# Keeping weight differences in device memory instead of making them again for every chunk

## The chip, the core and the metric

The kernel runs on one core of one Trainium2 chip. The metric is the device time of one execution in microseconds (us). The kernel before takes 1067.56 us, the median of three runs (1067.38 to 1067.63).

## The reference, cut to what matters

Linear attention without a softmax, with a root-mean-square norm per head, is followed by a gated feed-forward block. All tensors are float32 except the three weight matrices, which arrive as float64 and are converted at the start. There are 8 batches of 8 heads, 576 positions each, heads of width 64; the feed-forward block sees 4608 tokens of width 512 and has 1536 hidden units.

```python
kv  = np.einsum('bhsd,bhse->bhde', k, v)
out = np.einsum('bhsd,bhde->bhse', q, kv)
out = out / np.sqrt(np.mean(out * out, axis=-1, keepdims=True) + 1e-06) * g_norm
x   = out.transpose(0, 2, 1, 3).reshape(4608, 512)
gate = 1.0 / (1.0 + np.exp(-(x @ w_gate)))
val  = x @ w_val
return gate * val @ w_out
```

## The kernel before

The 4608 tokens are worked through in nine chunks of 512, numbered 0 to 8. Chunk 0 uses ordinary matrix products while the weights arrive and are converted. Chunks 1 to 8 use a Strassen-Winograd scheme in both layers: seven products of half size in place of eight, in exchange for sums and differences of the operands. TensorE makes the products, VectorE and ScalarE combine them, and GpSimd makes the differences of the weights. The attention of a later batch is fed in between the products of the first layer.

The first layer of a chunk has six rounds (`NF2 = 6`). Round f treats two blocks of 128 hidden units, f and f + 6, here called `one` and `two`. The differences of the gate and value weights of a round (`tw`, four tiles per block, and `tw2`, four small ones for an inner Strassen step) are made by GpSimd in the round before, and this is done again in every chunk although the weights never change:

```python
def w_sums2(f):
    bf, bg = w["wg", f], w["wg", f + NF2]
    b11, b12, b21, b22 = bf[:, NK], bg[:, NK], bf[:, NK + 1], bg[:, NK + 1]
    for i, in0, in1 in ((1, b12, b11), (2, b22, 1), (4, b21, 2), (3, b22, b12)):
        tw2[i] = sums.tile([P, P], FP32, tag=f"tx{i}", name=f"tx{i}", bufs=1)
        nc.gpsimd.tensor_tensor(out=tw2[i], in0=in0, in1=..., op=ALU.subtract)

def w_sum(f, i):
    ...
    tw[f, i] = sums.tile([P, NK, P], FP32, tag=f"tw{i}", name=f"tw{i}")      # two buffers per tag
    nc.gpsimd.tensor_tensor(out=tw[f, i], in0=b[in0], in1=..., op=ALU.subtract)
```

A round, with the vector work left out (`pN` is one product of two 128x128x256 float32 matmuls, `small` one matmul of 128 columns; `tw` and `tw2` are what each reads; `slot()` is a place where a step of the attention is fed in):

```python
p1(one); p1(two); slot()                          # weights themselves
small(..., ones[:, NK]); small(..., ones[:, NK + 1])
p6(one)                                           # tw[f, 2]
small(..., tw2[2]); small(..., tw2[4])
p6(two); slot()                                   # tw[f + 6, 2]
small(..., tw2[3])
p5(one); slot()                                   # tw[f, 1]
p7(one)                                           # tw[f, 3]
small(..., tw2[1]); slot()
p7(two); p5(two); slot()                          # tw[f + 6, 3], tw[f + 6, 1]
if more:                                          # the next round's differences
    for k_ in (1, 2):
        w_sum(n, k_); w_sum(n + NF2, k_)
    w_sums2(n)
    for i in (n, n + NF2): w_sum(i, 3)
p4(one); small(...); p4(two); slot()              # tw[f, 4], tw[f + 6, 4]
if more:
    for i in (n, n + NF2): w_sum(i, 4)
p3(one); p3(two); slot()                          # weights themselves
```

The buffers are just enough for one round: the differences of the next round go into the places that `p5`, `p6`, `p7` and `p4` of this round have just read.

All loads and stores go through one queue, that of SyncE, in program order. Two of them matter here: the keys and values of a later batch, loaded at the end of each chunk's second layer, and the queries, each loaded when the queries before have been turned.

```python
def load_late(b):                                 # called after the second layer of chunk c, for b = c + 2
    if b >= B: return
    for n in range(NHP):                          # 4 x (k, v): 8 loads of 256 KB
        for name, src in (("k", k), ("v", v)):
            nc.sync.dma_start(out=..., in_=src[b, 2 * n:2 * n + 2, 0:S4]...)
    for i, src in enumerate((k, v)):              # 4 loads of 64 KB
        for r in range(2):
            nc.sync.dma_start(out=..., in_=src[b, NHP * r:NHP * r + NHP, S4:S]...)
```

Of the kernel before, what the change touches and what calls it, by code (L numbers as in the profile page):

```python
# [10 lines left out]
FP32 = mybir.dt.float32  # L11
# [4 lines left out]
ALU = mybir.AluOpType  # L16
# [4 lines left out]
def kernel(  # L21
# [11 lines left out]
    nc = tc.nc  # L33
# [4 lines left out]
    P = 128  # L38
# [89 lines left out]
    staged, w = {}, {}  # L128
# [206 lines left out]
    def slot():  # L335
        if fill:
            fill.popleft()()
# [138 lines left out]
    def gv_tile(c, f):  # L476
        gv[c, f] = hp.tile([P, G], FP32, tag="gv", name="gv")
        return gv[c, f]

    def sg_tile():  # L480
        return sb.tile([P, G], FP32, tag="sg", name="sg", bufs=5)
# [29 lines left out]
    def bank(i):  # L511
        return (psum_mm if i < 2 else psum).tile([P, 512], FP32, tag=f"mm{i}", name="mm")
# [15 lines left out]
    def take():  # L528
        i = free.popleft()
        return i, bank(i)[:, 0:GH]  # L530

    def give(i):
        free.append(i)
# [67 lines left out]
    for token in order.split():  # L601
        name = token.rstrip("0123456789.")
        n = [int(i) for i in token[len(name):].split(".")]
        f = n[0]
# [68 lines left out]
    NK = NMT // 2  # L673
    NF2 = NFT // 2
# [3 lines left out]
    sx, tw, s12, s4 = {}, {}, {}, {}  # L678


    sx2, tw2 = {}, {}
# [3 lines left out]
    def quarters(c):  # L685
        return {(i, j): xT[c][:, NK * (j - 1):NK * j, GH * (i - 1):GH * i] for i in (1, 2) for j in (1, 2)}
# [18 lines left out]
            lambda: tt(out=s[:, 2], in0=a12, in1=s[:, 1], op=ALU.subtract),  # L705
        ]

    def w_sums2(f):

        bf, bg = w["wg", f], w["wg", f + NF2]  # L710
        b11, b12, b21, b22 = bf[:, NK], bg[:, NK], bf[:, NK + 1], bg[:, NK + 1]
        for i, in0, in1 in ((1, b12, b11), (2, b22, 1), (4, b21, 2), (3, b22, b12)):
            tw2[i] = sums.tile([P, P], FP32, tag=f"tx{i}", name=f"tx{i}", bufs=1)
            nc.gpsimd.tensor_tensor(out=tw2[i], in0=in0, in1=tw2[in1] if isinstance(in1, int) else in1,  # L714
                                    op=ALU.subtract)

    def w_sum(f, i):
        b = {(j, n): w[name, f][:, NK * (j - 1):NK * j, :] for n, name in ((1, "wg"), (2, "wv")) for j in (1, 2)}
        tw[f, i] = sums.tile([P, NK, P], FP32, tag=f"tw{i}", name=f"tw{i}")
        in0, in1 = {1: ((1, 2), (1, 1)), 2: ((2, 2), 1), 3: ((2, 2), (1, 2)), 4: ((2, 1), 2)}[i]  # L720
        nc.gpsimd.tensor_tensor(out=tw[f, i], in0=b[in0], in1=b[in1] if isinstance(in1, tuple) else tw[f, in1],  # L721
                                op=ALU.subtract)

    def first_layer_fast(c):
        s, a, s2, ax = sx[c], quarters(c), sx2[c], quarters(c)[1, 2]

        def product(ps, wt, xs, new):
            for m in range(NK):
                nc.tensor.matmul(ps, wt[:, m, :], xs[:, m, :], start=(new and m == 0), stop=(m == NK - 1),  # L729
                                 skip_group_check=True)  # L730

        def small(ps, wt, xs, new):
            nc.tensor.matmul(ps, wt, xs, start=new, stop=True, skip_group_check=True)  # L733


        def p1(d):
            d["ia"], d["pa"] = take()
            product(d["pa"], d["bg"][:, 0:NK], a[1, 1], True)

        def p1_out(d):  # L740
            d["u"] = d["sg"] = sg_tile()
            nc.scalar.copy(out=d["sg"][:, h2], in_=d["pa"])  # L742

        def p6(d):
            d["ib"], d["pb"] = take()
            product(d["pb"], tw[d["f"], 2], s[:, 1], True)
            d["h"] = gv_tile(c, d["f"])
            tt(out=d["h"][:, h1], in0=d["pb"], in1=d["sg"][:, h2], op=ALU.add)  # L748

        def u_sum(d, ps):  # L750

            tt(out=d["h"][:, h2], in0=ps, in1=d.pop("u")[:, h2], op=ALU.add)  # L752
            d["u"] = d["h"]

        def p5(d, i):
            d["ic"], d["pc"] = i, bank(i)[:, 0:GH]
            product(d["pc"], tw[d["f"], 1], s[:, 0], True)
            u_sum(d, d["pc"])

        def p7(d):  # L760
            product(d["pb"], tw[d["f"], 3], a[2, 1], False)
            u_sum(d, d["pb"])

        def p4(d):
            product(d["pb"], tw[d["f"], 4], a[2, 2], False)
            tt(out=d["sg"][:, h2], in0=d["pb"], in1=d["sg"][:, h2], op=ALU.add)  # L766
            nc.scalar.activation(out=d["sg"][:, h2], in_=d["sg"][:, h2], func=AF.Sigmoid)  # L767
            give(d["ib"])

        def p3(d):  # L770
            product(d["pc"], d["bv"][:, NK:], s[:, 2], False)
            tt(out=d["h"][:, h1], in0=d["pc"], in1=d["h"][:, h1], op=ALU.add)
            give(d["ic"])

        def end(d, h):
            tt(out=d["h"][:, h], in0=d["h"][:, h], in1=d["sg"][:, h], op=ALU.mult)  # L776

        for f in range(NF2):
            one, two = ({"f": i, "bg": w["wg", i], "bv": w["wv", i]} for i in (f, f + NF2))
            more = f + 1 < NF2 or c + 1 < NG  # L780
            n = (f + 1) % NF2
            ones, twos = one["bg"], two["bg"]

            p1(one)
            p1_out(one)
            p1(two)
            slot()


            i_d = free[2]  # L790
            del free[2]
            pd = bank(i_d)
            small(pd[:, q1], ones[:, NK], ax[:, 0, q1], True)
            g1 = one["sg"]
            nc.scalar.copy(out=g1[:, q1], in_=pd[:, q1])

            p1_out(two)
            g2 = two["sg"]
            small(one["pa"][:, q1], ones[:, NK + 1], ax[:, 1, q1], False)
            p6(one)  # L800
            small(pd[:, q1], tw2[2], s2[:, 1], False)
            nc.scalar.copy(out=g2[:, q1], in_=pd[:, q1])
            small(one["pa"][:, q2], tw2[4], ax[:, 1, q2], False)
            p6(two)
            slot()
            small(pd[:, q1], tw2[3], ax[:, 0, q2], False)
            nc.scalar.copy(out=g1[:, q2], in_=pd[:, q1])
            nc.scalar.copy(out=g2[:, q2], in_=pd[:, q1])  # L808
            nc.gpsimd.tensor_tensor(out=g2[:, h1], in0=g2[:, h1], in1=g2[:, h2], op=ALU.add)  # L809
            tt(out=g1[:, h1], in0=one["pa"], in1=g1[:, h1], op=ALU.add)  # L810
            nc.scalar.activation(out=g1[:, h1], in_=g1[:, h1], func=AF.Sigmoid)
            p5(one, two["ia"])
            slot()
            p7(one)
            pe = bank(i_d)
            small(pe[:, q1], tw2[1], s2[:, 0], True)
            tt(out=g2[:, q2], in0=pe[:, q1], in1=g2[:, q2], op=ALU.add)
            slot()
            p7(two)
            p5(two, one["ia"])  # L820
            slot()

            if more:
                for k_ in (1, 2):
                    w_sum(n, k_)
                    w_sum(n + NF2, k_)
                w_sums2(n)
                for i in (n, n + NF2):
                    w_sum(i, 3)
            p4(one)  # L830
            small(pe[:, q1], twos[:, NK + 1], s2[:, 2], False)
            tt(out=g2[:, q1], in0=pe[:, q1], in1=g2[:, q1], op=ALU.add)
            nc.scalar.activation(out=g2[:, h1], in_=g2[:, h1], func=AF.Sigmoid)
            p4(two)
            give(i_d)
            slot()
            if more:
                for i in (n, n + NF2):
                    w_sum(i, 4)

            end(one, h2)
            p3(one)
            end(two, h2)
            h_sum(c, f)
            p3(two)
            slot()
            end(one, h1)
            end(two, h1)
            h_sums(c, f)

    def h_sum(c, f):
        one, two = gv[c, f], gv[c, f + NF2]
        s12[c, f] = s = hp.tile([P, G], FP32, tag="gv", name="s12")
        tt(out=s[:, h1], in0=one[:, h2], in1=two[:, h2], op=ALU.add)
# [191 lines left out]
            fill.append(lambda: fill.extendleft(reversed(x_sums(c))))  # L1046

    sums = ctx.enter_context(tc.tile_pool(name="sums", bufs=2, side="right"))
    for n in (1, 2, 3, 4):
        for f in (0, NF2):  # L1050
            w_sum(f, n)
    w_sums2(0)
    fill.extend(x_sums(1))
    for t in range(G // P):
        for f in range(NFT - 2, NFT):
# [23 lines left out]
    for c in range(1, NG):  # L1079
        if c + 1 < B:  # L1080
            steps = feed(c + 1)
            if c == 1:

                i = 4
# [38 lines left out]
```

## Time and profile before

| What | Value |
|---|---|
| Time, median of 3 runs | 1067.56 us |
| Span of the profiled execution | 1066.2 us |
| TensorE busy | 1058.0 us, 99% of the span |
| VectorE busy | 740.6 us, 69% |
| GpSimd busy | 587.5 us, 55% |
| ScalarE busy | 307.2 us, 29% |
| Moved by DMA | 65.05 MB, 61 GB/s over the span |
| Granted TensorE clock | 1.000 |

How to read it: the busy time of TensorE is the union of the intervals of its matmul records. Matmuls are pipelined and their ends are modelled, so a busy share of 99% does not by itself say that nothing waits; the distances between the starts of matmuls do. The chain of waits names what ended last, step by step. A float32 matmul leaves two records in the trace. In the tables by line, the name ahead of `<-` is the tile that is written, the names after it those that are read, and `x` gives the count; tiles of converted weights show under the name `gv` or `w`. SPq is the DMA queue of SyncE.

### The profile page before, as it was taken

The numbers are of one execution on the slowest core, as the hardware profiler recorded it, in microseconds if no ns is written. First come the engines' busy times: TensorE is split into PE (matmuls) and PEld (weight loads), VectorE is DVE, ScalarE is ACT, GpSimd is POOL, SyncE is SP. The second block draws the span as 40 slices with busy tenths as digits, with TensorE's granted clock in tenths as the row PEclk, the third lists the DMA queues.
The fourth block names the chain that finished last, engine by engine and source line by source line (L and its number), as shares of the span: only waits on it lengthen the run. The fifth ranks groups of instructions, "written<-read, shape, count | busy, mean of one in ns | idle before, by whom it ended". The sixth has DMA issues, their size and how long they took to land.

```text
span 1066.2 us, 20718 instructions
## 1 busy us (share of the span) xinstructions
PE 1058.0 (99%) x7766; PEld 887.8 (83%) x7766; DVE 740.6 (69%) x1545; ACT 307.2 (29%) x737; POOL 587.5 (55%) x966
## 2 busy tenths in 40 slices
PE   8999999999999999999999999999999999999998
PEld 7644448888988898889888898889888988898887
DVE  4887776995678647884679467855787477827751
ACT  4654323331243214240333124311432022102210
POOL 0000035878366927784667736792678277847720
PEclk9999999999999999999999999999999999999999
DMA  9944601002400131011301150014000200010001
GB/s 254 263 158 158 239 20 38 12 13 57 141 1 23 43 102 55 23 35 47 117 13 27 41 141 8 16 50 135 14 24 24 62 1 1 1 38 4 1 1 40
DMA packets 70563, 65.05 MB, mean 61 GB/s; under 512 B 25152, under 2 KB 64448, under 8 KB 70464
## 3 DMA queue, kind: packets, MB, share of 16 engines
q1 hardware_dynamic: 70112, 63.66, 21.4%
q8 instruction: 62, 1.02, 0.4%
q14 instruction: 37, 0.30, 0.1%
q10 hardware_dynamic: 352, 0.07, 0.0%
HBM read 47.19 MB, written 9.44 MB: 53 GB/s over the span
## 4 chain that ended last, share of the span: by engine, by line
PE 98%; DMA 1%; SPq 1%; issue 0%; DVE 0%
PE mm L729 47%; PE mm L894 17%; PE mm L557 7%; PE mm L733 7%; PE mm L953 6%; PE mm L654 4%; PE mm L1004 3%; PE at L395 2%; PE at L354 1%; DMA v<-in_v_dram 1%; PE at L557 1%; PE two L261 0%; PE two L291 0%; PE two L318 0%; PE two L272 0%; SPq L87 0%
## 5 line engine op out<-in xcount | busy, mean ns | idle before, releaser
L721 POOL TENSOR_TENSOR tw<-gv 128x256 f32<-128x256 f32 x192 | 158.6, 836 | 258.0 <-DVE w L202 146.1
L729 PE MATMUL mm<-xT,tw 128*128 128x256 f32 x768 | 199.5, 382 | 0.0
L729 PE MATMUL mm<-sx,tw 128*128 128x256 f32 x768 | 197.4, 380 | 0.0
L721 POOL TENSOR_TENSOR tw<-gv,tw 128x256 f32<-128x256 f32 x192 | 153.4, 819 | 0.0
L729 PEld LDWEIGHTS mm<-xT,tw 128*128 128x128 f32 x768 | 136.6, 190 | 19.3 <-issue 3.8
L729 PEld LDWEIGHTS mm<-sx,tw 128*128 128x128 f32 x768 | 134.9, 191 | 12.3
L809 POOL TENSOR_TENSOR sg<-sg 128x256 f32<-128x256 f32 x48 | 35.1, 732 | 166.4 <-ACT sg L808 148.2
L776 DVE TENSOR_TENSOR gv<-gv,sg 128x256 f32<-128x256 f32 x192 | 110.7, 596 | 0.0
L742 ACT COPY sg<-mm 128x256 f32<-128x256 f32 x96 | 36.0, 375 | 242.7 <-PE mm L729 238.8
L729 PE MATMUL mm<-xT,gv 128*128 128x256 f32 x384 | 90.8, 379 | 0.0
L729 PE MATMUL mm<-sx,gv 128*128 128x256 f32 x384 | 90.7, 379 | 0.0
L767 ACT ACTIVATE sg<-sg 128x256 f32<-128x256 f32 x96 | 39.9, 416 | 149.7 <-DVE sg L766 149.7
L729 PEld LDWEIGHTS mm<-sx,gv 128*128 128x128 f32 x384 | 73.0, 190 | 9.9
L729 PEld LDWEIGHTS mm<-xT,gv 128*128 128x128 f32 x384 | 72.3, 190 | 10.0 <-issue 0.5
L557 PE MATMUL mm<-xT,gv 128*128 128x512 f32 x176 | 77.4, 593 | 0.0
L894 PE MATMUL mm<-w,s 128*128 128x256 f32 x336 | 73.7, 379 | 0.0
L894 PEld LDWEIGHTS mm<-w,s 128*128 128x128 f32 x336 | 63.8, 190 | 8.7
L752 DVE TENSOR_TENSOR gv<-mm,sg 128x256 f32<-128x256 f32 x96 | 39.9, 415 | 40.1 <-PE mm L729 39.1
L557 PEld LDWEIGHTS mm<-xT,gv 128*128 128x128 f32 x176 | 32.7, 190 | 37.4 <-issue 35.9
L766 DVE TENSOR_TENSOR sg<-mm,sg 128x256 f32<-128x256 f32 x96 | 40.4, 421 | 33.1 <-PE mm L729 32.9
L748 DVE TENSOR_TENSOR gv<-mm,sg 128x256 f32<-128x256 f32 x96 | 36.5, 411 | 37.6 <-PE mm L729 37.6
L714 POOL TENSOR_TENSOR tx<-gv,tx 128x128 f32<-128x128 f32 x96 | 54.6, 569 | 7.5
(156 smaller groups left out, 1907.5 us busy)
## 6 DMA issues: line engine op xcount, KB each, us to landing
out_dram<-sg SPq DMA_DIRECT2D x110, 64.0 KB, 1.7
q<-in_q_dram SPq DMA_DIRECT2D x24, 288.0 KB, 3.0
st<-in_moe_w_gate_dram SPq DMA_DIRECT2D x12, 512.0 KB, 4.6
st<-in_moe_w_val_dram SPq DMA_DIRECT2D x12, 512.0 KB, 5.6
st<-in_moe_w_out_dram SPq DMA_DIRECT2D x12, 512.0 KB, 4.3
kv<-in_k_dram SPq DMA_DIRECT2D x24, 256.0 KB, 5.0
kv<-in_v_dram SPq DMA_DIRECT2D x24, 256.0 KB, 5.0
xT<-xTs SPq DMA_DIRECT2D x48, 72.0 KB, 2.1
```

What stands on the lines that cost most here:

```text
L557: nc.tensor.matmul(self.ps[i], w[("wg", "wv")[i], self.f][:, m, :], xT[self.c][:, m, :], start=(m == 0), stop=(m == NMT - 1), skip_group_c ...
L654: nc.tensor.matmul(ps[t], gv[0, f][:, P * t:P * t + P], w["wo", f], start=(f == 0), stop=(f == NFT - 1), skip_group_check=True)
L714: nc.gpsimd.tensor_tensor(out=tw2[i], in0=in0, in1=tw2[in1] if isinstance(in1, int) else in1, op=ALU.subtract)
L721: nc.gpsimd.tensor_tensor(out=tw[f, i], in0=b[in0], in1=b[in1] if isinstance(in1, tuple) else tw[f, in1], op=ALU.subtract)
L729: nc.tensor.matmul(ps, wt[:, m, :], xs[:, m, :], start=(new and m == 0), stop=(m == NK - 1), skip_group_check=True)
L733: nc.tensor.matmul(ps, wt, xs, start=new, stop=True, skip_group_check=True)
L752: tt(out=d["h"][:, h2], in0=ps, in1=d.pop("u")[:, h2], op=ALU.add)
L766: tt(out=d["sg"][:, h2], in0=d["pb"], in1=d["sg"][:, h2], op=ALU.add)
L767: nc.scalar.activation(out=d["sg"][:, h2], in_=d["sg"][:, h2], func=AF.Sigmoid)
L776: tt(out=d["h"][:, h], in0=d["h"][:, h], in1=d["sg"][:, h], op=ALU.mult)
L894: nc.tensor.matmul(ps, hs[f], ws[:, f, :], start=(new and f == 0), stop=(f == NF2 - 1), skip_group_check=True)
L953: nc.tensor.matmul(ps, hs[j], ws[j], start=(new and j == 0), stop=(j == N3 - 1), skip_group_check=True)
```

## The change

In chunk 1 the differences are made by GpSimd as before, and each is also stored into device memory (`kept`, `kept2`). In every later chunk the same tiles are filled by a load from there. The two blocks of a round share one tile per kind (256 KB: 128 partitions of 2 KB), and the four inner differences share one (also 256 KB), so that a round needs five loads. The places in the program where the differences are made, and where they are now loaded, are the same, and so is the amount of buffer: two blocks in one tile with one buffer, instead of one block per tile with two. The change takes the repeated work off GpSimd.

```diff
-    def w_sums2(f):
+    def w_sums2(c, f):
+        t = sums.tile([P, 4, P], FP32, tag="tx", name="tx", bufs=1)
+        tw2.update({i: t[:, i - 1] for i in (1, 2, 3, 4)})
+        if c > 1:
+            nc.sync.dma_start(out=t, in_=kept2[f])
+            return
         ...
-            tw2[i] = sums.tile([P, P], FP32, tag=f"tx{i}", name=f"tx{i}", bufs=1)
             nc.gpsimd.tensor_tensor(out=tw2[i], in0=in0, in1=..., op=ALU.subtract)
+        nc.sync.dma_start(out=kept2[f], in_=t)
-    def w_sum(f, i):
-        tw[f, i] = sums.tile([P, NK, P], FP32, tag=f"tw{i}", name=f"tw{i}")
+    def w_sum(c, f, i):
+        t = sums.tile([P, 2, NK, P], FP32, tag=f"tw{i}", name=f"tw{i}", bufs=1)
+        for e in range(2):
+            tw[f + NF2 * e, i] = t[:, e]
+        if c > 1:
+            nc.sync.dma_start(out=t, in_=kept[i - 1, f])
+            return
-        nc.gpsimd.tensor_tensor(out=tw[f, i], ...)
+        for g in (f, f + NF2):
+            nc.gpsimd.tensor_tensor(out=tw[g, i], ...)
+        nc.sync.dma_start(out=kept[i - 1, f], in_=t)
     ...
             if more:                              # cn = c + (n == 0): the chunk of the next round
                 for k_ in (1, 2):
-                    w_sum(n, k_)
-                    w_sum(n + NF2, k_)
-                w_sums2(n)
-                for i in (n, n + NF2):
-                    w_sum(i, 3)
+                    w_sum(cn, n, k_)
+                w_sums2(cn, n)
+                w_sum(cn, n, 3)
     ...
             if more:
-                for i in (n, n + NF2):
-                    w_sum(i, 4)
+                w_sum(cn, n, 4)
     ...
+    kept  = kept_pool.tile([4, NF2, P, 2, NK, P], FP32, name="kept")      # in device memory
+    kept2 = kept_pool.tile([NF2, P, 4, P], FP32, name="kept2")
```

More of the change, by code (lines that the diff above doesn't have):

```diff
@@ L712, in w_sums2 @@
         for i, in0, in1 in ((1, b12, b11), (2, b22, 1), (4, b21, 2), (3, b22, b12)):
-            tw2[i] = sums.tile([P, P], FP32, tag=f"tx{i}", name=f"tx{i}", bufs=1)
             nc.gpsimd.tensor_tensor(out=tw2[i], in0=in0, in1=tw2[in1] if isinstance(in1, int) else in1,
                                     op=ALU.subtract)
-    def w_sum(f, i):
-        b = {(j, n): w[name, f][:, NK * (j - 1):NK * j, :] for n, name in ((1, "wg"), (2, "wv")) for j in (1, 2)}
-        tw[f, i] = sums.tile([P, NK, P], FP32, tag=f"tw{i}", name=f"tw{i}")
-        in0, in1 = {1: ((1, 2), (1, 1)), 2: ((2, 2), 1), 3: ((2, 2), (1, 2)), 4: ((2, 1), 2)}[i]
-        nc.gpsimd.tensor_tensor(out=tw[f, i], in0=b[in0], in1=b[in1] if isinstance(in1, tuple) else tw[f, in1],
-                                op=ALU.subtract)
+        nc.sync.dma_start(out=kept2[f], in_=t)
[6 more added lines that the diff above has]
+            return
+        in0, in1 = {1: ((1, 2), (1, 1)), 2: ((2, 2), 1), 3: ((2, 2), (1, 2)), 4: ((2, 1), 2)}[i]
+        for g in (f, f + NF2):
+            b = {(j, n): w[name, g][:, NK * (j - 1):NK * j, :] for n, name in ((1, "wg"), (2, "wv")) for j in (1, 2)}
+            nc.gpsimd.tensor_tensor(out=tw[g, i], in0=b[in0], in1=b[in1] if isinstance(in1, tuple) else tw[g, in1],
+                                    op=ALU.subtract)
+        nc.sync.dma_start(out=kept[i - 1, f], in_=t)
     def first_layer_fast(c):
@@ L781, in first_layer_fast @@
             n = (f + 1) % NF2
+            cn = c + (n == 0)
             ones, twos = one["bg"], two["bg"]
@@ L1048 @@
     sums = ctx.enter_context(tc.tile_pool(name="sums", bufs=2, side="right"))
+    kept_pool = ctx.enter_context(tc.tile_pool(name="kept_pool", bufs=1, space=bass.MemoryType.DRAM))
+    kept = kept_pool.tile([4, NF2, P, 2, NK, P], FP32, name="kept")
+    kept2 = kept_pool.tile([NF2, P, 4, P], FP32, name="kept2")
     for n in (1, 2, 3, 4):
-        for f in (0, NF2):
-            w_sum(f, n)
-    w_sums2(0)
+        w_sum(1, 0, n)
+    w_sums2(1, 0)
     fill.extend(x_sums(1))
```

## The prediction

> **What bounds the kernel now.** I read the busy shares first, then the chain of waits, then the list of who waited for whom, and last the order of time inside one round.
>
> ```profile
> PE 1058.0 (99%) x7766; PEld 887.8 (83%) x7766; DVE 740.6 (69%) x1545; ACT 307.2 (29%) x737; POOL 587.5 (55%) x966
> PEclk9999999999999999999999999999999999999999
> ```
>
> The chain that ended last, by engine:
>
> ```profile
> PE 98%; DMA 1%; SPq 1%; issue 0%; DVE 0%
> ```
>
> TensorE alone carries the chain, at full clock. GpSimd is not in it. The groups by line show GpSimd's work, and what its idle time waited for:
>
> ```profile
> L721 POOL TENSOR_TENSOR tw<-gv 128x256 f32<-128x256 f32 x192 | 158.6, 836 | 258.0 <-DVE w L202 146.1 <-PE mm L729 111.8
> L721 POOL TENSOR_TENSOR tw<-gv,tw 128x256 f32<-128x256 f32 x192 | 153.4, 819 | 0.0
> ```
>
> Read the releasers: GpSimd waits 111.8 us for TensorE to let go of the tiles, in 47 waits. In TensorE's own list of waits the only one for GpSimd is 1.4 us for the identity matrix at the start. So GpSimd follows TensorE, and not the other way round.
>
> Is TensorE's 99% real? The order of time in round 2 to 3 of the last chunk:
>
> ```profile
> 987.58 1.03 PE L729 MATMUL mm<-xT,tw 128*128 128x256 f32 x4
> 988.45 1.89 PE L729 MATMUL mm<-sx,gv 128*128 128x256 f32 x8
> 990.18 1.89 PE L729 MATMUL mm<-xT,gv 128*128 128x256 f32 x8
> 991.90 0.61 PE L733 MATMUL mm<-xT,gv 128*128 128x128 f32 x4
> 992.35 1.03 PE L729 MATMUL mm<-sx,tw 128*128 128x256 f32 x4
> ...
> 999.51 1.03 PE L729 MATMUL mm<-xT,tw 128*128 128x256 f32 x4
> ```
>
> The first column is the start. Four records (one product) take 988.45 - 987.58 = 0.87 us, eight take 1.73: 0.216 us from start to start. The same product `p4(two)` starts 999.51 - 987.58 = 11.93 us later. A round has 12 products and 7 small matmuls: 48 x 0.216 + 14 x 0.11 = 11.9 us. Nothing is left between them. What does not shorten the matmuls themselves can't make this kernel much faster.
>
> **What the Trainium skill says.** "TensorE: Matmul & The Clock Gate", section "Wait — 56ns, not 53.3ns?", gives N/2.4 + about 2.5 ns from start to start for a warm matmul. For N = 512 that is 0.216 us, just what each record here shows, as if a record of 256 float32 columns streamed 512. So TensorE is at its floor. "SBUF — State Buffer", section "SBUF: two separate sides", says that VectorE with two SBUF inputs and GpSimd exclude each other on a shared pair of ports, and that DMA uses other ports. The trace agrees with the first: L776 on VectorE (two SBUF inputs) takes 380 ns at least, 543 in the median and 949 at most, while L748, which reads PSUM, takes 405 to 425. "DMA: Bandwidth & Descriptors", section "Queues, rings and completion order", says that each DMA engine takes its descriptors in ring order: a load waits behind what was issued before it. The trace agrees: key and value loads of 256 KB, issued twelve in a row, take 5.0 us to land in the median, query loads of 288 KB only 3.0.
>
> **The change, part by part.**
>
> *Removed.* Of 48 sets of differences 42 go. One set costs GpSimd (158.6 + 153.4)/48 = 6.5 us for L721 and 107.7/48 = 2.2 us for the small ones (L714: 54.6 + 31.2 + 21.9); 42 sets are 42 x 8.7 = 367 us. GpSimd should fall from 587.5 to about 220 us. None of it is on the path.
>
> *Relieved.* VectorE's two-SBUF-input operations get the ports to themselves. L776 would go from 596 ns mean to its least, 380: 192 x 0.216 = 41 us. L861, L862 (933 mean, 416 least) and L863, L854 give about 70 more. Times 42/48 that is some 95 us: VectorE from 741 to about 645 us. TensorE's weight loads wait for VectorE in only two places that this touches (2.3 us for L772, 1.2 us for L776), so I put down **-2 us**.
>
> *Added in chunk 1.* 30 stores of 256 KB (7.9 MB). GpSimd works as before and TensorE waits for nothing new; the stores are 1.3 MB in 12 us. **0 us**.
>
> *Added in chunks 2 to 8.* 42 x 5 = 210 loads of 256 KB, 55 MB. DMA is idle enough on average: 61 GB/s now, about 120 after. What counts is each round's deadline. In a round, the first tile can be issued when `p5(two)` has been read; the order is tw1, tw2, tx, tw3, and tw4 after `p4(two)`. TensorE needs tw2 first, at the next `p6(one)`. Between the two lie p4, p4, p3, p3, p1, p1 (6 x 0.864) and three small matmuls (3 x 0.22): **5.8 us**; the first small product of tx comes 0.9 us after that, tw1 another 1.5 later. Cost of the loads: a lone 288 KB query load lands in about 3.0 us, issues follow each other every 0.51 us (key and value loads), and in a dense burst the engines move 230 to 370 GB/s, say 330, so each 256 KB adds 0.8 us. tw1 lands at about 0.2 + 3.0 = 3.2 us, tw2 at 4.0, tx at 4.8. Slack 1.8 us: **hidden in an ordinary round**.
>
> *The round where it is not hidden.* In chunks 2 to 6 the first round holds the twelve key and value loads (2.3 MB) and a query load. They stand ahead of the loads for round 1 in the same queue. Chunk 6, SyncE's queue and DMA by the microsecond (last two columns: share of the DMA engines, GB/s), and TensorE's need:
>
> ```profile
> 743.87 1.27 SPq L119 DMA_DIRECT2D kv<-in_v_dram  x2
> 745.23 0.55 SPq L100 DMA_DIRECT2D q<-in_q_dram  x1
> ...
> 746.00:747.00 1.00, 1.00 (x8) 0.90 (x7) 1.00 (x3) 0.37 (x1) 1.00 (x3) 1.00 0.97 228
> 747.00:748.00 1.00, 1.00 (x8) 0.92 (x7) 1.00 (x2) 0.54 (x2) 1.00 (x2) 1.00 0.53 189
> 748.00:749.00 1.00, 1.00 (x8) 0.92 (x8) 1.00 (x3) 0.27 (x1) 1.00 (x2) 1.00 0.00 2
> ...
> 747.18 1.03 PE L729 MATMUL mm<-sx,tw 128*128 128x256 f32 x4
> ```
>
> The engines are busy with keys, values and queries until about 747.5. tw1 and tw2 come behind them, 0.5 MB at 330 GB/s = 1.6 us: tw2 is there at 749.1, and `p6(one)` wants it at 747.18. TensorE stands 1.9 us. The same reading for the other chunks (end of the burst + 1.6 against the start of `p6(one)` of round 1): chunk 2, 288.7 + 1.6 against 289.91, 0.4 us; chunk 3, 404.5 against 404.55, 1.6; chunk 4, 519.2 against 518.46, 2.3; chunk 5, 633.6 against 633.27, 1.9. tx arrives 0.8 us after tw2 and is wanted 0.9 us after it, so it adds nothing. Sum 0.4 + 1.6 + 2.3 + 1.9 + 1.9 = 8.1, with some tenths for the signal **+8.5 us**. Chunks 7 and 8 load no keys and values: nothing there.
>
> Sum: 1067.6 - 2 + 8.5 = **1074 us**.
>
> **The rivals.** (a) *The loads are late in every round.* Then SyncE's queue or the DMA rate takes GpSimd's place as the thing to wait for, and where GpSimd never held TensorE up, this would. Half a microsecond in 42 rounds is 21 us, 1089. For it: four loads are issued at once into a window of 5.8 us, and one queue in order also holds query loads that wait for VectorE. Against: 1.8 us of slack, and the query loads of rounds 3 and 4 are issued before `p5(two)`. (b) *All is hidden*: the keys and values land sooner, or the loads share the engines with them, and only the relief of VectorE is left, 1065 to 1067. Against: the burst ends within 1.5 us of TensorE's need in all five chunks. (c) *GpSimd was the bound in disguise* and over 2% is gained. Against: 0.216 us from start to start, and no wait of TensorE for GpSimd. (d) *A stall cools TensorE.* The page on TensorE (same title as above, section "The HAM clock gate") has the clock halved after an idle window of about 3.4 us. Stalls of 2 us stay below that; the clock here never leaves 9 tenths, so the trace can't say. Where stalls came to over 3.4 us, each would cost some us more.
>
> **Range and chances.** The low end is (b), 1066.5. The high end is twice the loss, or a tenth of (a) with it: 1084. Faster by over 2% needs 21 us out of a TensorE that waits for some 4 us: 0.01. Slower by over 2% needs (a): 0.06. The rest is within 2%.
>
> **What the profile after would show.** GpSimd about 220 us; L721 with 48 instructions; VectorE near 645 us, with L776 near 400 ns; DMA near 128 MB. TensorE's list of waits should hold a new entry, matmuls or weight loads of `tw` waiting for a DMA of `tw` or `tx` out of `kept`, five times, 0.4 to 2.5 us each, all at the start of round 1 of chunks 2 to 6. If it appears some 40 times, (a) is right; if it is missing, (b). The prediction is wrong if a 256 KB load out of device memory lands much later than a query load of that size, if the granted clock drops, or if VectorE does not speed up.

## The result, and the profile after

The changed kernel takes 1092.38 us in the median of four runs (1088.73 to 1093.46), the kernel before 1067.47 us on the same chip. The ratio is 1.0231, with a 95% interval of 1.0213 to 1.0249: slower by over 2%. The change cost 24.9 us; the prediction had 6.5.

The page of the changed kernel begins with the busy time of the engines and the granted clock:

```profile
PE 1065.1 (98%) x7766; PEld 896.9 (82%) x7766; DVE 668.1 (61%) x1545; ACT 307.5 (28%) x737; POOL 241.1 (22%) x462
PEclk9999999999999999999999989999999999999999
```

GpSimd lost 346 us of work and VectorE 72 us, and neither shows in the time. TensorE is busy for 7.1 us *longer* with the same 7766 instructions. One digit of the clock is an 8. The chain that ended last, by engine, now gives 5% to DMA, where it had 1%:

```profile
PE 92%; DMA 5%; DVE 2%; SPq 1%; issue 1%; DVEq 0%
```

The groups by line give the matmuls that read a weight difference, and VectorE's operation with two SBUF inputs (line 776 before, 789 now). The last column is the idle time ahead of the group and what ended it:

```profile
L742 PE MATMUL mm<-sx,tw 128*128 128x256 f32 x768 | 202.5, 387 | 17.4 <-DMA tw<-kept 17.4
L789 DVE TENSOR_TENSOR gv<-gv,sg 128x256 f32<-128x256 f32 x192 | 80.8, 442 | 0.0
```

TensorE's list of waits (total us, number, longest):

```profile
PE mm L742 <- DMA tw<-kept: 17.4, 5, 4.6
...
PE mm L635 <- POOL ident masks.py:199: 1.4, 1, 1.4
PE mm L746 <- DVE gv L785: 0.8, 3, 0.3
PE mm L742 <- DVE gv L761: 0.7, 3, 0.3
```

The last two entries are new as well: the kernel before has no wait of TensorE for VectorE in its list. All six stand in chunk 1, where the differences are made and stored, and they come back in every version below. Matched by the starts of the same matmuls in both traces, chunk 1 is 1.8 us longer.

There are five waits for a load of `tw`, and not forty. The order of time on TensorE shows where; the bracket is the idle time just before:

```profile
293.21 1.13 PE L742 MATMUL mm<-sx,tw 128*128 128x256 f32 x4 [1.72 <-DMA tw<-kept]
...
411.08 1.13 PE L742 MATMUL mm<-sx,tw 128*128 128x256 f32 x4 [2.77 <-DMA tw<-kept]
...
529.38 2.08 PE L742 MATMUL mm<-sx,tw 128*128 128x256 f32 x4 [4.16 <-DMA tw<-kept]
...
650.22 2.08 PE L742 MATMUL mm<-sx,tw 128*128 128x256 f32 x4 [4.57 <-DMA tw<-kept]
...
770.97 1.50 PE L742 MATMUL mm<-sx,tw 128*128 128x256 f32 x4 [4.17 <-DMA tw<-kept]
```

Each is `p6(one)` in round 1 of chunks 2 to 6. Look at the second column as well: after the two shorter waits the four records take 1.13 us, after the three longer ones up to 2.08 us. The windows of one microsecond around the third wait say why. The columns are the window, its length, busy shares of TensorE, its weight loads, VectorE, ScalarE and GpSimd, then the granted clock, the share of the DMA engines and GB/s:

```profile
528.00:529.00 1.00, 0.00 (x0) 0.00 (x0) 0.00 (x0) 0.00 (x0) 0.00 (x0) 1.00 1.06 352
529.00:530.00 1.00, 0.62 (x2) 0.54 (x3) 0.00 (x0) 0.00 (x0) 0.00 (x0) 0.62 0.86 295
530.00:531.00 1.00, 1.00 (x4) 0.82 (x3) 0.00 (x0) 0.00 (x0) 0.00 (x0) 0.50 0.18 70
531.00:532.00 1.00, 1.00 (x6) 0.91 (x5) 0.42 (x1) 0.08 (x1) 0.00 (x0) 0.50 0.01 4
532.00:533.00 1.00, 1.00 (x5) 0.88 (x5) 0.00 (x0) 0.18 (x1) 0.00 (x0) 0.67 0.00 0
533.00:534.00 1.00, 1.00 (x7) 0.90 (x7) 0.46 (x2) 0.34 (x2) 0.00 (x0) 1.00 0.00 0
```

While TensorE stands still in this wait the DMA engines are full. When it starts again its clock is halved and stays so for 3.4 us, in chunk 5 for twice as long. Lost clock times busy share, summed over such windows, gives 1.6, 2.7 and 1.7 us for chunks 4, 5 and 6: 6.0 us. So two things carry most of the loss: **17.4 us of waits and about 6.0 us of half clock**.

### The profile page after: what moved, and what is told of

It reads as the page before. It is cut to its first block, busy times and chain, and to the rows that moved or that the text cites. A ratio compares the mean times of both kernels' runs of the same rounds, so it can differ in the third digit from the quotient of the medians.

```text
span 1091.7 us, 20481 instructions
## 1 busy us (share of the span) xinstructions
PE 1065.1 (98%) x7766; PEld 896.9 (82%) x7766; DVE 668.1 (61%) x1545; ACT 307.5 (28%) x737; POOL 241.1 (22%) x462
## 4 chain that ended last, share of the span: by engine, by line
PE 92%; DMA 5%; DVE 2%; SPq 1%; issue 1%; DVEq 0%
PE mm L742 43%; PE mm L905 17%; PE mm L557 7%; PE mm L746 6%; PE mm L964 6%; PE mm L654 4%; PE mm L1015 3%; PE at L395 2%; DMA tw<-kept 2%; DMA kv<-in_k_dram 2%; PE at L354 1%; DMA v<-in_v_dram 1%; PE at L557 1%; DVE gv L789 1%; PE two L261 0%
## 5 line engine op out<-in xcount | busy, mean ns | idle before, releaser
L742 PE MATMUL mm<-sx,tw 128*128 128x256 f32 x768 | 202.5, 387 | 17.4 <-DMA tw<-kept 17.4
L742 PEld LDWEIGHTS mm<-sx,tw 128*128 128x128 f32 x768 | 137.6, 195 | 31.3 <-DMA tw<-kept 18.3
L761 DVE TENSOR_TENSOR gv<-mm,sg 128x256 f32<-128x256 f32 x96 | 40.3, 423 | 114.5 <-PE mm L742 109.5
L789 DVE TENSOR_TENSOR gv<-gv,sg 128x256 f32<-128x256 f32 x192 | 80.8, 442 | 0.0
L765 DVE TENSOR_TENSOR gv<-mm,sg 128x256 f32<-128x256 f32 x96 | 40.6, 423 | 46.5 <-PE mm L742 40.7
L765 DVE TENSOR_TENSOR gv<-mm,gv 128x256 f32<-128x256 f32 x96 | 40.7, 424 | 28.1 <-PE mm L742 26.9
L733 POOL TENSOR_TENSOR tw<-gv 128x256 f32<-128x256 f32 x24 | 20.0, 853 | 162.2 <-DVE w L202 145.9
L894 POOL TENSOR_TENSOR gv<-gv 128x128 f32<-128x128 f32 x105 | 44.7, 455 | 1.6 <-PE mm L905 1.2
```

The lines of the kernel that those rows point to most:

```text
L894: nc.gpsimd.tensor_tensor(out=o[i][j], in0=u0, in1=u1, op=ALU.add if i == 1 and not weights else ALU.subtract)
```

## The experiments

All times are medians, and each ratio is to the kernel before on the same chip. Line numbers move by one or two between kernels.

### Round 1 made on the core

Is the late round the whole of it? Here GpSimd makes the differences of that one round in chunks 2 to 6; the other 37 sets are loaded.

```diff
-        if c > 1:
+        if c > 1 and not (f == 1 and c <= 6):                    # the same for tx
             nc.sync.dma_start(out=t, in_=kept[i - 1, f])
```

> As the changed kernel, but the differences for round 1 of chunks 2 to 6 are made by GpSimd again, and not loaded; all other rounds still load (185 loads in place of 210). Theory A (only the five loads behind the burst of keys, values and queries cost time, 17.4 us of standing still, and the halved clock that follows the long ones costs about 6 more): the five waits vanish, the clock is 1.000, and the time is 1065 to 1068 us. Rival B (the traffic of 55 MB or the stores slow the kernel in all rounds): most of the loss stays, 1080 us or more.

Measured: 1066.36 us, ratio 0.9992 (0.9984 to 1.0000). TensorE's list of waits holds no DMA any more:

```profile
PE mm L635 <- POOL ident masks.py:199: 1.4, 1, 1.4
PE mm L748 <- DVE gv L787: 0.8, 3, 0.3
PE mm L744 <- DVE gv L763: 0.8, 3, 0.3
```

The clock is 1.000. Five sets out of 42 carry the whole loss, and no matmul waits for one of the other 37. Chunk 1 costs its 1.8 us here too, in the six waits for VectorE; less waiting elsewhere makes up for them, and the net gain is 0.6 us. Whether the stores or the new order of GpSimd's work delays VectorE in chunk 1, no run separates.

### What stands behind the tile: nothing, or one load

The waits were 9.3 us longer than predicted. Part of the burst that keeps `tw2` away was loads issued *behind* it. In these two runs they are taken away in round 1 of chunks 2 to 6: in the first, GpSimd makes tx, tw3 and tw4 there, in the second only tw3 and tw4. (`tw2` here and below is the second of the four differences, as in the prediction.)

```diff
-        if c > 1:
+        if c > 1 and not (f == 1 and c <= 6 and i in (3, 4)):    # first run: the same for tx
             nc.sync.dma_start(out=t, in_=kept[i - 1, f])
```

> What is open: in the changed kernel the tile that TensorE wants first in the late round is there about a microsecond later than the bytes ahead of it in the queue account for. Here, in round 1 of chunks 2 to 6 only the first two differences (tw1, tw2) are loaded; tx, the third and the fourth are made by GpSimd, as before the change. What stands ahead of tw2 in the queue is the same, what is issued behind it is gone. Theory A (the loads issued behind share the DMA engines with tw2 while it is in flight, and so hold it up): the waits of TensorE for DMA fall from 17.4 us to about 11.6, the clock stays whole in some more chunks, time 1078 to 1085. Theory B (tw2 is late by its own path: the order of the queue, the wait of an issue for a completion signal of an earlier load, the landing itself): the waits stay within 1.5 us of 17.4, time 1089 to 1094.

> As the run with only two loads, but the inner differences (tx) are loaded too; only the third and fourth are made by GpSimd in round 1 of chunks 2 to 6. Theory A (what is issued behind tw2 shares the engines with it): one load of 256 KB is left behind tw2 in place of two in flight, so the waits lie between the two, about 13 to 16 us, time 1082 to 1089. Theory B (tw2 is late by its own path): 17.4 us within 1.5, 1089 to 1094. If tx itself becomes the tile waited for, the wait stands at the small products, 0.9 us after the first.

Measured: 1090.21 us (ratio 1.0207, 1.0182 to 1.0232) with waits of 16.3 us, and 1089.95 us (1.0216, 1.0199 to 1.0234) with 14.9 us. Theory A needed 11.6 us with nothing behind, and less there than with one load behind; neither came. The 14.9 us of the second run lie inside what A gave, but its time doesn't, and the order of the two is wrong for A. The first run fits theory B in both numbers. What stands behind `tw2` is not what makes it late. The lower sum of the second run goes with an earlier issue: against the moment at which TensorE begins to wait, SyncE issued `tw2` 3.4 us earlier there than in the first, in the five rounds together. With nothing behind it, the first run shows how a burst ends. Windows of half a microsecond, chunk 6:

```profile
767.00:767.50 0.50, 0.00 (x0) 0.00 (x0) 0.00 (x0) 0.00 (x0) 0.00 (x0) 1.00 0.91 309
767.50:768.00 0.50, 0.00 (x0) 0.00 (x0) 0.00 (x0) 0.00 (x0) 0.00 (x0) 1.00 0.19 66
768.00:768.50 0.50, 0.00 (x0) 0.00 (x0) 0.00 (x0) 0.00 (x0) 0.00 (x0) 1.00 0.07 25
768.50:769.00 0.50, 0.00 (x0) 0.00 (x0) 0.00 (x0) 0.00 (x0) 0.00 (x0) 1.00 0.02 8
769.00:769.50 0.50, 0.28 (x1) 0.28 (x2) 0.00 (x0) 0.00 (x0) 0.16 (x1) 1.00 0.00 0
```

At 767.5 us the engines are all but done. Then a share of 0.07, about one engine of sixteen, goes on for another microsecond, and TensorE starts at 769.22. From the end of the full share to the restart it is 1.7 us here, and 1.1, 1.4, 1.2 and 1.4 us in chunks 2 to 5: 6.8 us in all. The prediction had the tile usable as soon as the bulk of its bytes was through. "DMA: Bandwidth & Descriptors", section "Anatomy of one DMA — SWDGE (gpsimd) path", puts most of a transfer's fixed cost after its last byte. It speaks of transfers issued by GpSimd; for these, issued by SyncE, the trace shows 0.4 to 0.9 us from the last moment at which any engine moves bytes to the restart, and stragglers for up to 1.2 us before.

### The tile that is wanted first, loaded first

```diff
-                for k_ in (1, 2):
-                    w_sum(cn, n, k_)
-                w_sums2(cn, n)
+                w_sum(cn, n, 2)              # only where loaded; chunk 1 as before
+                w_sums2(cn, n)
+                w_sum(cn, n, 1)
```

> As the changed kernel, but each round's loads are issued in the order in which TensorE needs them: tw2, tx, tw1, tw3, tw4. Theory A with loads that land in the order of issue: tw2 is there one load of 256 KB sooner, 0.9 to 1.1 us; five waits shorten by about 1 us each and the clock drops shrink or vanish, 1082 to 1087 us. Rival D (the loads in flight share the engines and land close together whatever their order): no change, 1091 to 1093 us.

Measured: 1085.69 us, ratio 1.0166 (1.0144 to 1.0188). TensorE's list of waits:

```profile
PE mm L742 <- DMA tw<-kept: 11.9, 5, 3.4
```

One place earlier in the queue is worth (17.4 - 11.9)/5 = 1.1 us. The prediction had 0.8 us for a place of 256 KB. The clock is still halved after three of the five waits (3.45, 3.05 and 2.38 us), for 10.2 us in all where it was 13.7; so the drops shrank only a little.

### A clock kept warm

TensorE multiplies the identity with itself, ten times, just before the wait in chunks 4 to 6; the results are never read. This adds work and takes none away.

```diff
+            if f == 1 and 4 <= c <= 6:
+                spare = at_ps()
+                for _ in range(10):
+                    nc.tensor.matmul(spare[:, 0, 0:P], ident, ident, start=True, stop=True)
             p6(one)
```

> As the changed kernel, with ten matmuls of 128x128 by the identity, whose result nobody reads, in front of the first product that waits in round 1 of chunks 4 to 6: 2.2 us of work inside waits of 4.2 to 4.6 us. Theory A (the clock halves because TensorE stands still for too long): standing still falls to about 2.2 us each, the clock stays at 1.000, and added work makes the kernel faster by about 6 us, 1086 us. Rival C (the clock drop has another cause, or costs nothing): the time stays at 1092 us.

Measured: 1086.55 us, ratio 1.0187 (1.0158 to 1.0217): 5.8 us less than the changed kernel, for 7.2 us of matmuls that compute nothing. The waits fall to 10.0 us because these matmuls fill the rest. Chunk 4 again, in the order of time and in windows:

```profile
524.67 2.40 PE L817 MATMUL at<-ident 128*128 128x128 f32 x20
...
529.71 1.13 PE L742 MATMUL mm<-sx,tw 128*128 128x256 f32 x4 [2.65 <-DMA tw<-kept]
```

```profile
530.00:531.00 1.00, 1.00 (x6) 0.65 (x6) 0.05 (x1) 0.00 (x0) 0.00 (x0) 1.00 0.57 209
531.00:532.00 1.00, 1.00 (x8) 0.92 (x8) 0.37 (x1) 0.27 (x1) 0.00 (x0) 1.00 0.04 14
```

TensorE restarts at 529.71, as late as before, but with a whole clock. So the half clock was a cost of its own, of the size of the 6.0 us read from the windows. Not all of it is gone: in chunk 2, where nothing was added, a wait of only 1.99 us now halved the clock, and only some 0.7 us after matmuls ran again. The last section shows why.

### Another queue

If the late tile stands behind keys and values in SyncE's queue, another queue should free it. Two were tried, ScalarE's and GpSimd's.

```diff
-            nc.sync.dma_start(out=t, in_=kept[i - 1, f])
+            nc.scalar.dma_start(out=t, in_=kept[i - 1, f])     # second run: nc.gpsimd.dma_start
```

> As the changed kernel, but the loads of the differences go through ScalarE's DMA queue and no longer stand behind the keys, values and queries in SyncE's. Theory A1 (the order of the one queue is what makes them late): they share the engines with the burst half and half, tw1 and tw2 need about 3.7 us after a start of 2 us, against 5.8 us; waits of 1 us or less, no clock drop, 1068 to 1075 us. Rival A2 (the engines are simply full for that long): waits of 3 us or more stay, 1085 us or more.

> As the changed kernel, but the loads of the differences are issued by GpSimd on its own queue, where they neither stand behind the burst in a queue nor wait for one of the eight completion signals that SyncE's loads take in turn (which the loads on ScalarE's queue still did), and block no engine that TensorE needs. Theory A1 (place in the queue): they share the engines with the burst from the end of p5 on, waits of 1 us or less, 1067 to 1075 us. Rival A2 (the engines are full, sharing gives too little): waits of 2 to 4 us stay, 1080 us or more. A third way: descriptors made by GpSimd itself come slowly enough to delay ordinary rounds too, over 1095 us.

ScalarE's queue: 1096.08 us, ratio 1.0271 (1.0254 to 1.0288), slower than the changed kernel. ScalarE in the order of time:

```profile
528.72 0.42 ACT L780 ACTIVATE sg<-sg 128x256 f32<-128x256 f32 x1 [9.20 <-DMA tw<-kept]
```

ScalarE did nothing for 9.20 us, since a load that it had to issue waited. In the trace the transfers issued by SyncE and ScalarE use one shared set of eight completion signals in turn, so that an issue waits until the transfer eight places earlier has landed, and here that was a key, value or query load of the other queue. Behind the held issue stood a sigmoid, behind it VectorE, and behind that TensorE:

```profile
PE mm L746 <- DVE gv L785: 17.7, 9, 4.7
```

The wait has the same size under another name. GpSimd's queue: 1074.93 us, ratio 1.0074 (1.0056 to 1.0091). TensorE's list of waits:

```profile
PE mm L742 <- DMA tw<-kept: 4.7, 4, 1.4
...
PE mm L746 <- DMA tx<-kept: 0.2, 1, 0.2
```

4.9 us are left of 17.4, at a clock of 1.000, and GpSimd is busy for 353.4 us, of which 113.4 us are the issuing of its 210 loads. So the place behind keys and values in SyncE's queue is the cause of most of the wait. This place has two sides, the bytes ahead and the completion signals that an issue waits for; both are gone here, and no run separates them. The profiled execution took 1072.18 us, 5.0 us above before, which is about the waits; the other three took 1074.31 to 1077.86 us, and why they took longer isn't known.

### The burst behind the urgent loads

All 210 loads stay, all in SyncE's queue, but keys and values are issued in round 0 after the load of tw4 for round 1, instead of at the end of the second layer. The attention that uses them starts three idle steps later.

```diff
-        load_late(c + 2)
+        put_off.append(c + 2)
 ...
                 w_sum(cn, n, 4)
+            if put_off:
+                load_late(put_off.pop())
 ...
-            steps += [(PE, idle)] * 6
+            steps += [(PE, idle)] * 9
```

> As the changed kernel with all its 210 loads, but the burst of keys and values is issued in the first round of a chunk, behind the loads for round 1, and no longer at the end of the second layer ahead of them; the products of the keys and values come three steps later in the feed. Theory A (it is the place of the five loads behind 2.6 MB that costs, not the number of loads or bytes): no waits of TensorE for the differences, clock 1.000, 1065 to 1069 us. Rival B (bytes in that stretch are too many in any order): the wait moves to the keys and values, 1075 us or more.

Measured: 1065.70 us, ratio 0.9985 (0.9979 to 0.9992), faster than the changed kernel and, by 0.15%, than the one before. SyncE's queue around the start of chunk 4:

```profile
512.59 0.82 SPq L729 DMA_DIRECT2D tw<-kept  x2
513.46 0.42 SPq L714 DMA_DIRECT2D tx<-kept  x1
513.92 1.78 SPq L729 DMA_DIRECT2D tw<-kept  x2
515.75 0.43 SPq L114 DMA_DIRECT2D kv<-in_k_dram  x1
516.28 0.41 SPq L114 DMA_DIRECT2D kv<-in_v_dram  x1
```

The five weight loads go out first, and the keys and values after them. TensorE's list of waits has no DMA of `kept`, and the clock is 1.000. The amount of data is that of the changed kernel; the order alone was the cost.

### How much room an ordinary round has

On top of the kernel with round 1 made on the core, stores of 256 KB of a weight tile into device memory were put into the queue in each of the other 37 sets. They add traffic and compute nothing. First they stood ahead of the five loads of a set, two or four of them:

```diff
+                for e in range(2):                        # second run: 4
+                    nc.sync.dma_start(out=extra[(2 * f + e) % 8], in_=w2[:, f])
                 w_sum(cn, n, 1)
                 w_sum(cn, n, 2)
```

> As the kernel that makes the differences of round 1 again, with two stores of 256 KB into unused device memory issued ahead of the loads in each round that loads: 0.5 MB at some 350 GB/s is 1.5 us of the slack of an ordinary round. Theory A (slack of about 1.8 us): hidden or nearly so, 1066 to 1072 us. Rival E (ordinary rounds stand at the edge): half a microsecond or more in each of 30 rounds, 1080 us or more.

> The same with four stores, 1 MB and 3 us ahead of the loads, issued over 2 us. Theory A: the slack of 1.8 us is used up, the first load that is needed comes 1 to 1.5 us late in 30 rounds: 1095 to 1115 us. If the slack is above 3 us, it stays at 1066 us.

Measured: 1070.22 us (ratio 1.0029, 1.0019 to 1.0040) and 1075.18 us (1.0074, 1.0058 to 1.0089). As a measure of the room both runs failed: these stores wait for nothing TensorE does, so they mostly went out while the queue was idle. With four, the stores of one round were issued from 439.15 to 441.47 us, and its loads only from 442.55 us. TensorE waits in one round per chunk alone (8.0 us in five waits), where a query load held the stores up until just before the loads. So they were moved between tw1, which does wait for TensorE, and tw2:

```diff
                 w_sum(cn, n, 1)
+                for e in range(2):                        # second run: 4
+                    nc.sync.dma_start(out=extra[(2 * f + e) % 8], in_=w2[:, f])
                 w_sum(cn, n, 2)
```

> The two stores ahead of the loads did not wait for TensorE and went out while the queue was idle, so they measured nothing of the slack. Here two stores of 256 KB stand between the load of tw1, which waits for the end of p5, and that of tw2, in each round that loads (30 of them with no second layer between). Slack of 1.8 us or more in an ordinary round: 0.5 MB at 330 to 390 GB/s is 1.4 to 1.6 us, hidden, 1066 to 1070 us. No slack: 1.5 us in 30 rounds, 1105 us or more.

> The same with four stores between tw1 and tw2: 2.8 to 3.2 us against a slack of 1.8 to 2.0, so tw2 comes about 1 us late in 30 rounds: 1085 to 1105 us, with some 30 or more waits of TensorE for the differences. Slack above 3 us: 1066 to 1070 us and no such waits.

Measured: 1087.95 us (1.0199, 1.0170 to 1.0227) and 1122.81 us (1.0535, 1.0499 to 1.0571). TensorE's list of waits, first with two stores:

```profile
PE mm L744 <- DMA tw<-kept: 10.1, 16, 1.7
```

and with four:

```profile
PE mm L744 <- DMA tw<-kept: 42.3, 30, 2.8
```

The list holds idle time above 0.15 us. With two, 16 of the 37 sets are late by more than that, by 0.6 us in the mean; with four, 30 are, by 1.4 us. At the prediction's 0.8 us for 256 KB, two are 1.6 us and four are 3.2, so the sets that are late had 1.0 to 1.8 us of room and the others more: an ordinary round has room for about two such loads, and it differs from round to round. The prediction worked out 1.8 us for all. That room is why TensorE waits for none of the 37 sets. With two stores the span of the profiled run grew by 18.7 us, and the waits are only 10.1. A restart costs 0.26 us beyond its wait: TensorE's idle time is counted from the end of the last record, 0.16 us after the next would have started (a row of four records lasts 1.03 us, and the next row starts after 0.87), and the first row after a wait lasts 1.13 us. In 16 waits that is 4.2 us. The starts of the same matmuls put the other 4.4 us into rounds where `tw2` or tx is late by some 0.15 us or less, so at two stores most rounds are at the edge.

## Why the prediction was wrong in size and right in place

**TensorE bounds, and GpSimd was not a disguised bound: right.** Without 346 us of GpSimd's work the best version gains 1.5 us. Rival (c) falls.

**What was removed: right within 10%.** GpSimd is at 241 us, predicted 220. VectorE is at 668 us, predicted 645: its operation with two SBUF inputs came down from 596 to 442 ns in the mean, and not to its least of 380. The two versions that wait for no load gain 0.6 and 1.5 us; predicted 2. That this comes so near is partly luck, since chunk 1 takes 1.8 us off it.

**Ordinary rounds: right; chunk 1: wrong by 1.8 us.** The first experiment leaves no wait for a load in 37 sets, and the last pair finds room of about 1 to 2 us in them where the prediction had 1.8. Rival (a) falls. For chunk 1 the prediction had 0 us and "TensorE waits for nothing new"; it waits six times for VectorE.

**Where and how often TensorE waits: right.** Five waits, round 1 of chunks 2 to 6, for `tw`. Rival (b) falls.

**How long it waits: wrong, and this is the step that failed.** The prediction's term was "end of the burst + 1.6" against the start of `p6(one)`, 8.1 us in all, with 0.4 us for the signal; measured 17.4. The version where nothing follows the tile, with waits of 16.3 us, lets the term be taken apart:

- Until the full share of the DMA engines ends, with the burst and both tiles through: 9.5 us, predicted 8.1. A place of 256 KB is worth 1.1 us in this burst and not 0.8.
- From there to TensorE's restart: 6.8 us, predicted 0.4. This is what was mis-sized most.

In the changed kernel the loads behind cover the tail, so there it can't be read; that it is as long there is inferred from waits that hardly differ (16.3 and 17.4 us). Why single engines finish a microsecond after the others stays open. The prediction also let loads follow each other every 0.51 us. In chunk 5 of the changed kernel SyncE held `tw2` back until a key load had landed, and issued it when TensorE already stood (from 645.65 us on). The first line is from its order of time, the second from its list of waits for that moment:

```profile
645.81 0.34 SPq L728 DMA_DIRECT2D tw<-kept  x1
SPq L728 <- DMA kv<-in_k_dram: 0.7, 1, 0.7
```

From its issue to the restart `tw2` took 3.8 to 5.0 us in the five rounds, where a lone query load lands in 3.0. How much of the waits hangs on the late issue, no run shows.

**The clock: wrong.** Rival (d) was named and put aside with "Stalls of 2 us stay below that". The waits came out twice as long, and so it cost 6.0 us, most of which the version kept warm gives back. But a wait of 2 us wasn't safe either, as the last section shows.

**The sum.** The profiled spans differ by 1091.7 - 1066.2 = 25.5 us. 17.4 are waits, 6.0 half clock, 1.3 the five restarts at 0.26 us and 1.8 chunk 1; about 1 us goes the other way. The range failed upwards because its high end doubled the waits, which was just enough for them, and let nothing follow from them.

## What to carry to other kernels

A load that must be in time is judged by the worst round and not by the mean: add up what stands ahead of it in its queue, at the rate of a crowded moment, and add the tail from the last bulk of bytes to the first use, here over a microsecond. Ahead of all other cures comes the order: bulk transfers whose use is far off belong behind the small urgent ones, which here turned a loss of 24.9 us into a gain of 1.5 with the same bytes. And when a predicted wait of the bounding engine comes near 2 us, put the price of a halved clock into the high end of the range.

## What the runs showed of the hardware that was not expected

**What halves TensorE's clock.** Five runs (the changed kernel, kept warm, tw2 first, and the two with less behind the tile) have five such waits each. After the five of up to 1.72 us the clock was never halved, after the twelve of 3.05 us and more always, and between 1.99 and 2.77 us in three of eight (1.99, 2.02 and 2.38 us yes; 2.10, 2.21, 2.59, 2.65 and 2.77 no). Length alone doesn't decide there; the place of the wait does. A half clock lasts 3.41 us or twice that, and within a trace all changes of the clock lie whole multiples of 3.41 us apart. So the clock is set for stretches of 3.41 us that do not begin with a wait. Cut at these times, the wait of 1.99 us in the version kept warm and the longer one of 2.77 us in the changed kernel look like this (columns as above; the first after the length is TensorE's busy time):

```profile
289.93:293.34 3.41, 1.42 (x9) 1.16 (x8) 0.95 (x3) 0.54 (x2) 0.00 (x0) 1.00 1.02 331
293.34:296.75 3.41, 3.41 (x12) 2.90 (x12) 0.45 (x2) 0.27 (x1) 0.00 (x0) 0.50 0.10 37
```

```profile
406.36:409.77 3.41, 1.96 (x12) 1.58 (x10) 2.18 (x7) 0.91 (x3) 0.00 (x0) 1.00 1.01 287
409.77:413.19 3.42, 2.11 (x11) 1.71 (x12) 0.42 (x1) 0.27 (x1) 0.00 (x0) 1.00 0.72 238
413.19:416.60 3.41, 3.41 (x42) 3.03 (x42) 1.90 (x5) 0.85 (x3) 0.73 (x1) 1.00 0.01 2
```

The shorter wait falls into one stretch and leaves TensorE 1.42 us of work in it: the next stretch has half the clock. The longer one is split over two, with 1.96 and 2.11 us of work, and the clock stays whole. In all 14 traces, from 60 us on and up to the last matmuls, no stretch at whole clock in which TensorE was idle for up to 0.53 of the time was followed by a halved one, and 22 of the 23 stretches with 0.55 or more were. The shortest wait that halved the clock was 1.87 us (the run with four stores between). "TensorE: Matmul & The Clock Gate", section "The HAM clock gate", names an idle window of about 3.4 us and calls it free-running. The traces agree with its length and that it runs on by itself; read as a least length of a wait, as the prediction did, it is contradicted.

**The halving can come late.** The wait of 1.99 us ended at 292.64 us, but its stretch only at 293.34. So the halving came 0.7 us after matmuls ran again, and then cost 1.7 us.

**Loads on two queues hold each other up.** ScalarE stood 9.20 us to issue a load, with its own compute behind it. In this run, then, loads issued from a compute engine stopped it until loads of another queue had landed.
